# Unread products in front of the early attention steps: a number for each kind of step in place of one number for all

## The chip, the cores and the metric

The kernel runs on one core of a Trainium2 chip. The metric is the time of one execution on the device in microseconds (us), the median of several runs. TensorE (PE) does the matmuls, VectorE (DVE), ScalarE (ACT) and GpSimd (POOL) the elementwise work, SyncE (SP) issues most transfers. TensorE's clock is granted at one of two levels, 1.2 or 2.4 GHz; the profile shows it as 0.50 or 1.00.

## The reference

Eight batches of eight heads, 576 tokens each, head size 64. Each head gets two attentions, whose sum is the output: a pooled one over means of four tokens (144 x 144 scores), each result repeated four times, and a local one, in which a token sees those less than four places away. The heads side by side give 4608 tokens of 512 numbers, which go through two matrices with h * cos(h) between them.

```python
q_d = q.reshape(B, H, Sd, factor, D).mean(axis=3)      # the same for k and v; factor 4
out_up = np.repeat(sm_attn(q_d, k_d, v_d), factor, axis=2)
mask = np.abs(pos[:, None] - pos[None, :]) < factor
scores = np.where(mask, scale * q @ k.T, -1e9)         # softmax over the last axis -> attn
x = (out_up + attn @ v)                                # then (tokens, 512)
h = x @ w_in                                           # 512 -> 2048
return (h * np.cos(h)) @ w_out                         # 2048 -> 512
```

## The kernel before

Two heads make a pair, so a batch has four pairs; a pair goes through these steps on TensorE. `u_s` makes scores: local ones (L743 adds the mask through an identity, L748 multiplies small blocks of 32 x 32) and pooled ones (L757, L760). After a softmax on the other engines `u_t` transposes the pooled weights, in two halves (L829, L830). `u_pv` multiplies by the values: pooled (L975, 8 matmuls) and local (L987, many small matmuls of 24 columns). Float32 operands make two records of one such matmul in the trace.

The sums of both go into `x`, in tiles of 384 tokens; tile 0 needs batch 0 alone, tiles 1 and 2 need batch 1. Then `gemm1` multiplies a tile by one of 16 weight blocks (L1026, three float16 products for each of four parts of 512), `cosine` makes h * cos(h) on ScalarE and VectorE, and `gemm2` (L1132) accumulates the output. Before a weight block can be used, `w_split` splits it into two float16 halves (L477 to L485 on ScalarE and VectorE), with a sum over all partitions by four tiny matmuls (L499, L500). `x_scale` does the like for `x` (reduction into `vm` at L557, matmuls L560 and L561); it needs the squares of all values of batches 0 and 1.

Batches 0 and 1 are early: their attention runs before there are any products of tiles. The order of the work on every engine is written out by a planner: `schedule` lays each operation with a given length onto its engine by a key, forwards and backwards eight times, and `mend` then changes keys at random, from a fixed seed, and keeps what makes the plan shorter. An operation with alternatives goes to the engine that would be done sooner (the sums of pooled values `u_vd`, L701 and L702, to GpSimd or VectorE). So other lengths change the order on all engines.

TensorE gets products that nobody reads (L1279): identity times identity, 256 columns, into a bank that is free at the time. They stand in front of an operation where the plan has a gap, up to 16 of them. In front of every TensorE operation of an early attention step there are at least `CFG["warm"][batch]` of them, 2 for both batches, if a bank is free; the planner adds 0.11 us of planned length for each.

Of the kernel before, what the change touches and what calls it, by code (L numbers as in the profile page):

```python
# [52 lines left out]
NEARLY = 2  # L53
# [16 lines left out]


CFG = dict(cold=6.8, queue=0.0, alttol=0.3, iters=8, mix=0.0, tabpen=3.2, lat=0.2, latself=0.05, latpe=0.25, late=0.17,
           fgap=0.4, f0=0.8, fend=300.0, warm=(2, 2), fstep=0.13)


class Buf:
# [11 lines left out]

class Op:
    __slots__ = ("eng", "dur", "fn", "tab", "deps", "sdeps", "now", "start", "end", "lat", "name", "arg", "preds", "succs",  # L90
                 "i", "fin", "alts", "boost", "tol")


class Plan:
# [16 lines left out]
        i = self.turns[tag] = self.turns.get(tag, -1) + 1  # L111
        return f"{tag}.{i % n}"

    def op(self, eng, dur, fn, r=(), w=(), pw=(), tab=None, after=(), lat=0.0, alts=(), tol=None):
        o = Op()
        o.tol = CFG["alttol"] if tol is None else tol
        o.alts = {eng: (dur, fn)}
        for e, d, f in alts:
            o.alts[e] = (d, f)
        o.eng, o.dur, o.fn, o.tab, o.now, o.lat, o.name = eng, dur, fn, tab, self.now, lat, self.name  # L120
        o.arg, o.boost = self.arg, self.boost
        o.deps, o.sdeps = list(after), []
        if eng == "PE" and self.name in ("u_s", "u_t", "u_pv") and self.arg[0] < NEARLY:
            o.alts[eng] = (dur + 0.11 * CFG["warm"][self.arg[0]], fn)
        for b in r:
            o.deps += b.w
        for b in w:
            o.deps += b.r + b.w
        for b in pw:
            o.deps += b.r  # L130
        for b in r:
            b.r.append(o)
            b.acc.append(o)
        for b in w:
            b.w, b.r = [o], []
            b.allw.append(o)
            b.acc.append(o)
        for b in pw:
            b.w.append(o)
            b.allw.append(o)  # L140
            b.acc.append(o)
        self.ops.append(o)
        return o
# [210 lines left out]
def attn_ffn_kernel(ctx: ExitStack, tc: tile.TileContext, qT, kT, vdn, vl, w_in, w_out, out):  # L354
# [8 lines left out]
    pl = Plan()  # L363
# [44 lines left out]
    for t in range(NT):  # L408
        r = (t - TS) % (NX - 1)
# [195 lines left out]
    def h_scale(g, c0, c1, v):  # L605
# [6 lines left out]
        for c in range(c0, c1, n):  # L612
# [5 lines left out]
            for k in range(c, c + n):  # L618
# [14 lines left out]
                sml=([P, NBLK, BS], 4), smd=([P, NQG, SD], 3), ptd=([HD, 2, 2, SD], 2),  # L633
                xd=([P, SD], 2), xs=([P, S], 3))

    def ub(b, pr, name):
        return later(name, UNIT[name][0]) if b >= NEARLY and name in ("q", "k", "vl") else sb(name, UNIT[name][1], UNIT[name][0])
# [80 lines left out]
    def u_s(b, pr):  # L718
        pl.name = "u_s"
        u = st[(b, pr)]  # L720
        q, k_, qkd, qkg = u["q"], u["k"], u["qkd"], u["qkg"]
        early = b < NEARLY
        sml, smd = ub(b, pr, "sml"), ub(b, pr, "smd")
        banks = [bank(b, "s"), bank(b, "s")]
        loc, poo = pl.buf(None), pl.buf(None)
# [22 lines left out]
                            pe.matmul(to()[BS * w:BS * (w + 1), j - c.start], q.get()[hs, o:o + BS], k_.get()[hs, o:o + BS],  # L748
                                      start=not early, stop=not early or j == c.stop - 1)
        if early:  # L750
            pl.op("PE", 1.31, l_mm, r=[q, k_], pw=banks, w=[loc])

        def d_mm():
            to = [t() for _, _, _, t in cuts(gcut, SD)]
# [4 lines left out]
                hs = slice(64 * h, 64 * h + 64)  # L759
                pe.matmul(to[0][hs, 1], qkg()[hs, 0, SD - QG:], qkg()[hs, 1, :], start=True, stop=True)  # L760
        if early:
            pl.op("PE", 0.66, d_mm, r=[qkd], pw=banks, w=[poo])
        else:
            pl.op("PE", 1.62, lambda: (l_mm(), d_mm()), r=[q, k_, qkd], pw=banks, w=[loc, poo])

        n, m = NBLK * BS, NQG * SD
# [3 lines left out]
        for i, (k, c, w, src) in enumerate(cuts(lcut, BS)):  # L770
            if early:
                mx = pl.buf(None)
                using(k, "DVE", _dve(w), lambda c=c, src=src: dve.tensor_reduce(out=mxl.get()[:, c], in_=src(), axis=AX.X, op=ALU.max),
                      r=[loc], pw=[mxl], w=[mx])
                using(k, "DVE", _dve(w), lambda c=c, src=src: dve.tensor_tensor(
                    out=sml.get()[:, c], in0=src(), in1=wide(mxl.get()[:, c], BS), op=ALU.subtract), r=[loc, mx], pw=[sml])
            else:
                using(k, "DVE", _dve(w), lambda c=c, src=src: dve.tensor_tensor(out=sml.get()[:, c], in0=src(), in1=mask[:, c], op=ALU.add),
                      r=[loc], pw=[sml])
# [3 lines left out]
        for k, c, w, src in cuts(gcut, SD):  # L783
            using(k, "DVE", _dve(w), lambda c=c, src=src: dve.tensor_reduce(out=mxd.get()[:, c], in_=src(), axis=AX.X, op=ALU.max, negate=True),
                  r=[poo], pw=[mxd])
# [9 lines left out]
        o = pl.op("ACT", _act(n, False) + 1.2, exps, r=[poo], w=[mxd, sml, smd], pw=[su, part], tab="exp")  # L795
# [8 lines left out]
        for sm, f, size, bc in ((sml, sul, n, BS), (smd, sud, m, SD)):  # L804
            f = lambda e, sm=sm, f=f, bc=bc: lambda: e.tensor_tensor(out=sm.get(), in0=sm.get(), in1=wide(f(), bc), op=ALU.mult)
            alts = [("DVE", _dve(size), f(dve))]
# [8 lines left out]
    def u_t(b, pr):  # L815
        pl.name = "u_t"
        u = st[(b, pr)]
        sml, smd = u["sml"], u["smd"]
        ptd = ub(b, pr, "ptd")
        pl.op("DVE", _dve(NBLK * BS), lambda: dve.transpose(sml.get().rearrange("p c n -> p (c n)"), sml.get().rearrange("p c n -> p (c n)")),  # L820
              w=[sml])
        for kh in range(2):
            bk = bank(b, "t")

            def t_mm(kh=kh, bk=bk):
                ks = slice(kh * HD, (kh + 1) * HD)
                to = bk.get()[:HD, :2 * SD].rearrange("p (h n) -> p h n", h=2)
                for h in range(2):
                    pe.transpose(to[:, h, :SD - HQ], smd.get()[:SD - HQ, 2 * h, ks], ident[:SD - HQ, :SD - HQ])  # L829
                pe.transpose(to[:, :, SD - QG:], smd.get()[:, 1, ks], ident)  # L830
            pl.op("PE", 0.29, t_mm, r=[smd], w=[bk])
            evac(2 * SD, lambda kh=kh: ptd.get()[:, kh],
                 lambda bk=bk: bk.get()[:HD, :2 * SD].rearrange("p (a n) -> p a n", a=2), bk, ptd, scale=1.0)
        u["ptd"] = ptd
# [129 lines left out]
    def u_pv(b, pr):  # L964
        pl.name = "u_pv"
        u = st.pop((b, pr))
        sml, ptd, vd, vt, vdg = (u[n] for n in ("sml", "ptd", "vd", "vl", "vdg"))
        banks = [bank(b, "v") for _ in range(2)]
        poo, loc = pl.buf(None), [pl.buf(None) for _ in banks]
        xd, xs = ub(b, pr, "xd"), ub(b, pr, "xs")  # L970

        def d_mm():
            for kh in range(2):
                for h in range(2):
                    pe.matmul(banks[0].get()[64 * h:64 * h + 64, 2 * SD:3 * SD], vdg()[:, kh, 64 * h:64 * h + 64],  # L975
                              ptd.get()[:, kh, h, :], start=(kh == 0), stop=(kh == 1))
        if b < NEARLY:
            pl.op("PE", 0.64, d_mm, r=[vd, ptd], pw=[banks[0]], w=[poo])

        def l_mm():  # L980
            for a in range(NSEG // 2):
                for i in range(4):
                    for e in range(2):
                        for h in range(2):
                            r = slice(64 * h + 32 * e, 64 * h + 32 * e + 32)
                            o = (4 * a + i) * BQ
                            pe.matmul(banks[e].get()[64 * h:64 * h + 64, o:o + BQ], vt.get()[r, a, i, :], sml.get()[r, 4 * a + i, :BQ],  # L987
                                      start=True, stop=True)
        if b < NEARLY:
            pl.op("PE", 1.55, l_mm, r=[vt, sml], pw=banks, w=loc)  # L990
        else:
            pl.op("PE", 2.22, lambda: (d_mm(), l_mm()), r=[vd, ptd, vt, sml], pw=banks, w=loc + [poo])

        evac(SD, xd.get, lambda: banks[0].get()[:, 2 * SD:3 * SD], banks[0], xd, scale=0.25)
        xd.w[-1].deps += poo.w
        half = [pl.buf(None) for _ in range(2)]
        for e in range(2):
            pl.op("DVE", _dve(S // 2), lambda e=e: dve.tensor_tensor(
                out=xs.get().rearrange("p (a e n r) -> p a e n r", e=2, a=NSEG // 2, r=4)[:, :, e],
                in0=banks[e].get()[:, :12 * BQ].rearrange("p (a n r) -> p a n r", a=NSEG // 2, r=4),  # L1000
                in1=xd.get().rearrange("p (a e n) -> p a e n", e=2, a=NSEG // 2)[:, :, e].unsqueeze(3).broadcast_to(
                    [P, NSEG // 2, BQ, 4]), op=ALU.add), r=[banks[e], loc[e], xd], pw=[xs], w=[half[e]])
        x_out(b, pr, xs)
# [178 lines left out]
    for c in range(NC):  # L1182
        for k, d in (("i", 0.0), ("o", 0.2)):
            t = need[c - c % NF] + 0.4 * (c % NF) if c >= NF else need[c]
# [3 lines left out]
    for k in blocks:  # L1188
        i = min(i for i, s in enumerate(steps) if s[2:] + (s[0] >= TS,) == k)
# [29 lines left out]
    for i in range(len(steps) + LAG):  # L1219
        if i < len(steps):  # L1220
            t, c, c0, c1 = steps[i]
# [47 lines left out]
    with tc.manual_schedule():  # L1269
        constants()  # L1270
        for o in order:
            if o.eng == "PE" and o.start < CFG["fend"]:

                ahead = o.name in ("u_s", "u_t", "u_pv") and o.arg[0] == 0
                s = (last, 0.0, idle) if ahead else spare(last, o.start)
                early = o.name in ("u_s", "u_t", "u_pv") and o.arg[0] < NEARLY
                n = min(int((o.start - s[0] - CFG["fgap"]) / (0.23 if last < 5 else CFG["fstep"])), 16) if s else 0
                for _ in range(max(n, CFG["warm"][o.arg[0]] if early and s else 0)):
                    pe.matmul(s[2].get()[:, :2 * P], ident_b, ident_b.unsqueeze(1).broadcast_to([P, 2, P]), start=True, stop=True)  # L1279
                last = o.start + o.dur  # L1280
            made = o.fn()
            if size.get(o):
                room = AHEAD
                for prior, n in reversed(under):
                    room -= n
                    if room < 0:
                        tc.add_manual_dep(made.ins, prior.name, sync, reason="bytes under way")
                        break
                under.append((made.ins, size[o]))
# [35 lines left out]
```

## Time and profile before

| | us |
|---|---|
| three runs | 966.94, 966.71, 965.43; median 966.71 |
| the profiled execution | 967.24 |
| its span, first to last instruction | 965.5 |
| TensorE busy | 940.7 (97%) |
| VectorE busy | 792.6 (82%) |
| ScalarE busy | 616.9 (64%) |
| GpSimd busy | 374.2 (39%) |
| mean granted clock | 0.972 |

Busy time counts an engine as busy while one of its instructions runs, at whatever clock. A matmul at 1.2 GHz is a busy TensorE just as one at 2.4, so the share of busy time hides half-speed stretches; the granted clock shows them.

### The profile page before, as it was taken

What the parts mean: (1) busy time and instruction counts of PE and PEld (TensorE: products, weight loads), DVE (VectorE), ACT (ScalarE), POOL (GpSimd) and SP (SyncE); (2) the same over time, 40 slices, a digit from 0 to 9 for tenths busy, and PEclk for the clock granted to TensorE, in tenths of its full rate; (3) what the DMA queues carried; (4) which work ended last, traced back from release to release, by engine and by line L of the source; (5) the groups of instructions that cost most, each with busy time, mean ns of one, the idle gap of its engine ahead of it and who ended that gap; (6) DMA issues with size and microseconds to landing.
All of it is one profiled execution on the core that took longest, in us unless ns stands there. A gap on an engine that the chain in (4) does not pass through costs nothing.

```text
span 965.5 us, 29154 instructions
## 1 busy us (share of the span) xinstructions
PE 940.7 (97%) x12209; PEld 622.1 (64%) x12209; DVE 792.6 (82%) x1643; ACT 616.9 (64%) x1326; POOL 374.2 (39%) x515
## 2 busy tenths in 40 slices
PE   7899899999999999999999999999999999999998
PEld 5667555555565655655677676677777777676774
DVE  6865899899877776789998799898798889887774
ACT  3633688889786666557486576675467576665543
POOL 4542378566532322357742344351122233321010
PEclk9775899999999999999999999999999999999999
DMA  7851498976554541220110241130121110000000
GB/s 230 235 166 47 123 230 236 250 194 132 140 126 101 121 97 43 75 67 26 43 51 26 75 112 42 55 84 13 43 76 43 60 52 2 1 35 2 33 2 33
DMA packets 42732, 84.98 MB, mean 88 GB/s; under 512 B 4136, under 2 KB 14632, under 8 KB 42600
## 3 DMA queue, kind: packets, MB, share of 16 engines
q1 hardware_dynamic: 36120, 69.15, 22.5%
q0 software_dynamic: 6480, 13.96, 9.5%
q8 instruction: 96, 1.57, 0.7%
q14 instruction: 36, 0.29, 0.1%
HBM read 65.01 MB, written 18.09 MB: 86 GB/s over the span
## 4 chain that ended last, share of the span: by engine, by line
PE 85%; DVE 8%; issue 2%; ACT 2%; DMA 1%; POOL 0%; POOLq 0%; ACTq 0%; DVEq 0%; SPq 0%
PE bank L1132 34%; PE bank L1065 19%; PE bank L1026 13%; PE bank L987 5%; PE bank L748 3%; PE bank L1279 3%; PE bank L975 2%; PE bank L757 1%; DVE wv L483 1%; PE bank L829 1%; PE bank L760 1%; DVE wv L485 1%; DMA norm<-vdn 1%; PE bank L830 1%; DVE wv L481 1%
## 5 line engine op out<-in xcount | busy, mean ns | idle before, releaser
L1132 PE MATMUL bank<-wo,gh 128*128 128x512 f16 x996 | 296.2, 379 | 0.0
L443 POOL TENSOR_TENSOR gl<-tr,gh 128x384 f16<-128x384 f32 x92 | 93.3, 1014 | 248.3 <-ACT gh L1113 161.5
L1132 PE MATMUL bank<-wo,gl 128*128 128x512 f16 x498 | 188.6, 379 | 0.0
L1071 DVE TENSOR_TENSOR room<-room,bank 128x384 f32<-128x384 f32 x224 | 111.3, 499 | 46.3 <-PE bank L1065 38.3
L1132 PEld LDWEIGHTS <-gh 128*128 128x128 f16 x996 | 94.1, 98 | 77.1 <-issue 1.4
L1026 PEld LDWEIGHTS <-wi 128*128 128x128 f16 x960 | 94.5, 99 | 70.2 <-issue 4.3
L1065 PEld LDWEIGHTS <-wi 128*128 128x128 f16 x1344 | 114.7, 98 | 16.5 <-issue 1.0
L1110 ACT ACTIVATE tr<-tr,bhalf 128x384 f32<-128x384 f32 x166 | 100.5, 611 | 28.3 <-DVE tr L1108 26.3
L1065 PEld LDWEIGHTS <-room 128*128 128x128 f16 x1008 | 86.1, 98 | 17.8 <-issue 3.8
L1113 ACT ACTIVATE gh<-tr 128x384 f16<-128x384 f32 x128 | 66.1, 519 | 47.9 <-DVE tr L1111 33.9
L1132 PEld LDWEIGHTS <-gl 128*128 128x128 f16 x498 | 48.7, 98 | 58.8
L1111 DVE SCALAR_TENSOR_TENSOR tr<-tr,rho016True,room 128x384 f32<-128x384 f32 x112 | 74.1, 667 | 3.4 <-ACT tr L1110 2.4
L1026 PE MATMUL bank<-x0h,wi 128*128 128x384 f16 x256 | 69.9, 336 | 0.1
L1107 ACT ACTIVATE tr<-room,bquart,hs3016True 128x384 int32<-128x384 f32 x48 | 33.5, 704 | 43.4 <-DVE room L1071 43.1
L987 PEld LDWEIGHTS bank<-sml,vl 32*64 32x64 f32 x3072 | 53.3, 144 | 9.7 <-issue 6.3
L987 PE MATMUL bank<-sml,vl 32*64 32x24 f32 x3072 | 57.0, 220 | 2.2 <-issue 1.1
L1132 PE MATMUL bank<-wo,room 128*128 128x512 f16 x234 | 56.1, 379 | 0.0
L443 POOL TENSOR_TENSOR room<-room 128x256 f16<-128x256 f32 (+3 forms) x50 | 44.3, 928 | 24.8 <-ACT room L912 15.8
L443 DVE TENSOR_TENSOR gl<-tr,gh 128x384 f16<-128x384 f32 x74 | 47.0, 640 | 4.3 <-ACT gh L1113 2.9
L1107 ACT ACTIVATE tr<-room,bquart,hs2016True 128x384 int32<-128x384 f32 x48 | 33.0, 702 | 23.4 <-DVE room L1071 20.2
L1158 POOL DMA_DIRECT2D out<-ob x33 | 30.8, 1083 | 40.3 <-ACT ob L1149 20.5
L1279 PE MATMUL bank<-ident_b 128*128 128x256 bf16 x225 | 41.1, 314 | 3.7 <-POOL ident_b masks.py:199 3.7
(338 smaller groups left out, 2282.4 us busy)
## 6 DMA issues: line engine op xcount, KB each, us to landing
vl<-vl SPq DMA_DIRECT2D x32, 384.0 KB, 3.5
q<-qT SPq DMA_DIRECT2D x32, 292.0 KB, 4.0
k<-kT SPq DMA_DIRECT2D x32, 292.0 KB, 3.6
out<-ob SPq DMA_DIRECT2D x36, 256.0 KB, 2.1
out<-ob POOLq DMA_DIRECT2D x33, 256.0 KB, 6.7
wd<-w_in SPq DMA_DIRECT2D x16, 512.0 KB, 5.2
wd<-w_out SPq DMA_DIRECT2D x16, 512.0 KB, 4.7
norm<-vdn SPq DMA_DIRECT2D x24, 288.0 KB, 6.0
```

The source lines that it names most:

```text
L443: f = lambda e: lambda: e.tensor_tensor(out=out(), in0=in0(), in1=in1(), op=ALU.subtract)
L987: pe.matmul(banks[e].get()[64 * h:64 * h + 64, o:o + BQ], vt.get()[r, a, i, :], sml.get()[r, 4 * a + i, :BQ], start=True, stop=True)
L1026: pe.matmul(ph.get()[:, :m], w[:, i, kc, :], x[:, kc, :], start=(n == 0), stop=(n == 3 * KC - 1))
L1065: pe.matmul(to.get(), blk(a)[:, kc], x_parts(t)[b][0 if main else 1][:, i, kc], start=(n == 0), stop=(n == 5))
L1071: pl.op("DVE", _dve(n * HT), lambda: dve.tensor_tensor(out=out(), in0=wide(one.get()), in1=two(), op=ALU.add), r=r, w=w)
L1107: pl.op("ACT", _act(m, True, 2), lambda: act.activation(ti(), h(), AF.Identity, bias=bquart, scale=inv()), r=mine + [hp], w=[tr])
L1110: pl.op("ACT", _act(m, False, 1), lambda: act.activation(tr.get(), tr.get(), AF.Sin, scale=2.0 * PI, bias=bhalf), w=[tr], tab="sin")
L1111: pl.op("DVE", _dvs(m), lambda: dve.scalar_tensor_tensor(out=tr.get(), in0=tr.get(), scalar=rho(), in1=h(), op0=ALU.mult, op1=ALU.mult), r ...
L1113: pl.op("ACT", _act(m, False), lambda: act.activation(gh.get(), tr.get(), AF.Copy), r=[tr], w=[gh], alts=[("DVE", _dve(m / 2), lambda: dve ...
L1132: pe.matmul(o, (gh, gh, gl)[k].get()[:, sl], wo.get()[:, (0, 1, 0)[k]], start=(c == c0 and k == 0), stop=(c == c1 - 1 and k == 2))
L1158: pl.op("POOL", 1.0, lambda dst=dst, ob=ob: pool.dma_start(dst, ob.get(), accum_op=ALU.add), r=[ob], w=[part[(t, i)]], lat=6.0)
L1279: pe.matmul(s[2].get()[:, :2 * P], ident_b, ident_b.unsqueeze(1).broadcast_to([P, 2, P]), start=True, stop=True)
```

## The change

The number of unread products now hangs on the kind of step and no longer on the batch: local scores 2 (`l`), pooled scores 1 (`d`), each half of the transposes 1 (`t`), pooled values 1 (`vd`), local values 4 (`vl`). An operation carries its number as `warm`, and the planner adds the same 0.11 us for each. A pair had 12 at least and has 9. Gaps in the plan are filled as before.

```diff
-           fgap=0.4, f0=0.8, fend=300.0, warm=(2, 2), fstep=0.13)
+           fgap=0.4, f0=0.8, fend=300.0, fstep=0.13)
+WARM = {"l": 2, "d": 1, "t": 1, "vd": 1, "vl": 4}
...
-        if eng == "PE" and self.name in ("u_s", "u_t", "u_pv") and self.arg[0] < NEARLY:
-            o.alts[eng] = (dur + 0.11 * CFG["warm"][self.arg[0]], fn)
+        if warm:
+            o.alts[eng] = (dur + 0.11 * warm, fn)
...
-            pl.op("PE", 1.31, l_mm, r=[q, k_], pw=banks, w=[loc])
+            pl.op("PE", 1.31, l_mm, r=[q, k_], pw=banks, w=[loc], warm=WARM["l"])
...
-            pl.op("PE", 0.29, t_mm, r=[smd], w=[bk])
+            pl.op("PE", 0.29, t_mm, r=[smd], w=[bk], warm=WARM["t"] if b < NEARLY else 0)
...
-            pl.op("PE", 1.55, l_mm, r=[vt, sml], pw=banks, w=loc)
+            pl.op("PE", 1.55, l_mm, r=[vt, sml], pw=banks, w=loc, warm=WARM["vl"])
...
-                early = o.name in ("u_s", "u_t", "u_pv") and o.arg[0] < NEARLY
                 n = min(int((o.start - s[0] - CFG["fgap"]) / (0.23 if last < 5 else CFG["fstep"])), 16) if s else 0
-                for _ in range(max(n, CFG["warm"][o.arg[0]] if early and s else 0)):
+                for _ in range(max(n, o.warm if s else 0)):
```

In the order of instructions the line numbers of the changed kernel are two or three higher (L1281 for L1279, L990 for L987). TensorE, batch 1, where the first product of tile 0 stands (`x0h` and `wi` are its operands, `wq` the sums of weight block 1, `sml` and `vl` local values, `ptd` and `vsum` pooled ones). Before:

```order
L987 MATMUL bank<-sml,vl 64x24 x48
L499 MATMUL bank<-wq,ones 128x2
L500 MATMUL bank<-ones,tiny 128x2
...
L829 MATMUL bank<-ident,smd 72x96 x2
L830 MATMUL bank<-ident,smd 72x2x64
L1026 LDWEIGHTS wi_1040
L1026 MATMUL bank<-x0h,wi_1040 128x384
```

And now, from the last matmul of that product on:

```order
L1029 LDWEIGHTS wi_1044
L1029 MATMUL bank<-x0h,wi_1044 128x384
L502 MATMUL bank<-wq,ones 128x2
L503 MATMUL bank<-ones,tiny 128x2
...
L990 MATMUL bank<-sml,vl 64x24 x48
L1281 LDWEIGHTS ident_b
L1281 MATMUL bank<-ident_b 128x256
L978 MATMUL bank<-ptd,vsum 64x144 x4
```

The last pair's local values and the sums of block 1 stood ahead of the product, and stand behind it now; the pooled values of that pair stand behind it in both.

VectorE in batch 0, up to the reduction into `vm` (`wd` and `vsum` are the sums of pooled values of one pair). Before:

```order
L820 STREAM_TRANSPOSE sml<-sml 128x384
L701 TENSOR_TENSOR wd<-wd 72x512
L702 TENSOR_TENSOR vsum<-wd 72x256
L651 COPY ptd<-bank 72x288
L651 TENSOR_SCALAR xd<-bank 128x144
L701 TENSOR_TENSOR wd<-wd 72x512
L702 TENSOR_TENSOR vsum<-wd 72x256
L998 TENSOR_TENSOR xs<-bank,xd 128x3x96
L557 TENSOR_REDUCE vm<-vq_126 128x1
```

And now:

```order
L654 COPY ptd<-bank 72x288
L823 STREAM_TRANSPOSE sml<-sml 128x384
L704 TENSOR_TENSOR wd<-wd 72x512
L705 TENSOR_TENSOR vsum<-wd 72x256
L654 TENSOR_SCALAR xd<-bank 128x144
L560 TENSOR_REDUCE vm<-vq_126 128x1
```

Two pairs of batch 1 were summed here on VectorE, now it is one; the other stands on GpSimd. The first sum of `xs` stands behind the reduction now.

## Rows read from the trace of the kernel before

**Rows 1.** The page's forty slices: PE busy in tenths, granted clock in tenths.

```profile
PE   7899899999999999999999999999999999999998
PEclk9775899999999999999999999999999999999999
```

**Rows 2.** Stretches: length, busy of PE, PEld, DVE, ACT, POOL, clock, DMA.

```profile
34.70:44.90 10.20, 9.47 (x188) 7.34 (x188) 8.59 (x23) 4.36 (x12) 6.45 (x11) 0.50 0.82 241
44.90:48.30 3.40, 3.14 (x102) 2.26 (x94) 1.58 (x4) 1.41 (x4) 0.94 (x3) 1.00 0.86 259
48.30:55.10 6.80, 6.74 (x185) 4.68 (x178) 6.30 (x14) 2.47 (x5) 6.33 (x10) 0.50 0.71 232
55.10:65.40 10.30, 8.42 (x220) 6.18 (x220) 8.53 (x35) 4.53 (x18) 4.42 (x7) 1.00 0.74 229
65.40:75.60 10.20, 9.93 (x82) 6.09 (x83) 3.87 (x13) 3.94 (x16) 1.26 (x3) 0.50 0.02 5
75.60:79.00 3.40, 3.40 (x154) 2.75 (x154) 1.83 (x6) 1.15 (x7) 0.44 (x1) 1.00 0.02 5
79.00:99.50 20.50, 19.19 (x302) 13.16 (x297) 9.86 (x28) 6.80 (x17) 4.74 (x10) 0.50 0.16 54
99.50:113.20 13.70, 9.52 (x76) 6.84 (x75) 12.20 (x31) 8.28 (x17) 2.49 (x7) 1.00 0.31 83
```

**Rows 3.** Chain of waits, 35.4 to 101 us: start, length, what.

```profile
63.05 1.88 issue
...
76.31 1.64 PE bank L987 x96
...
79.29 0.83 issue
...
84.24 0.43 PE bank L1279 x2
84.67 2.70 PE bank L987 x96
...
95.93 3.78 PE bank L1026 x12
...
100.68 0.30 ACT xd L650
```

**Rows 4.** TensorE's timeline: start, length of the group, what.

```profile
30.15 0.33 PE L829 MATMUL bank<-ident,smd 96*72 96x96 f32 x2
...
30.43 0.38 PE L1279 MATMUL bank<-ident_b 128*128 128x256 bf16 x2
...
65.94 0.61 PE L1279 MATMUL bank<-ident_b 128*128 128x256 bf16 x2
66.61 0.54 PE L829 MATMUL bank<-ident,smd 96*72 96x96 f32 x2
...
67.15 0.63 PE L1279 MATMUL bank<-ident_b 128*128 128x256 bf16 x2
...
101.06 0.33 PE L1026 MATMUL bank<-x0h,wi 128*128 128x384 f16 x1
...
103.01 1.91 PE L1279 MATMUL bank<-ident_b 128*128 128x256 bf16 x16
```

**Rows 5.** Two further stretches, columns as in rows 2.

```profile
18.10:35.40 17.30, 13.70 (x371) 10.25 (x369) 17.13 (x38) 13.05 (x39) 11.94 (x11) 0.98 0.81 224
...
65.94:99.93 33.99, 32.41 (x500) 21.70 (x495) 15.55 (x45) 12.07 (x39) 6.43 (x12) 0.56 0.10 34
```

**Rows 6.** VectorE's timeline before the reduction into vm.

```profile
32.71 0.67 DVE L701 TENSOR_TENSOR wd<-wd 72x512 f32<-72x512 f32 x1
33.42 1.44 DVE L702 TENSOR_TENSOR vsum<-wd 72x256 f32<-72x256 f32 x1
...
35.16 0.14 DVE L557 TENSOR_REDUCE vm<-vq 128x1 f32<-128x8 f32 x1
```

More of the change, by code (lines that the diff above doesn't have):

```diff
@@ L90 @@
     __slots__ = ("eng", "dur", "fn", "tab", "deps", "sdeps", "now", "start", "end", "lat", "name", "arg", "preds", "succs",
-                 "i", "fin", "alts", "boost", "tol")
+                 "i", "fin", "alts", "boost", "tol", "warm")
 class Plan:
@@ L112, in turn, with op @@
         return f"{tag}.{i % n}"
-    def op(self, eng, dur, fn, r=(), w=(), pw=(), tab=None, after=(), lat=0.0, alts=(), tol=None):
+    def op(self, eng, dur, fn, r=(), w=(), pw=(), tab=None, after=(), lat=0.0, alts=(), tol=None, warm=0):
         o = Op()
+        o.warm = warm
         o.tol = CFG["alttol"] if tol is None else tol
@@ L761, in u_s @@
         if early:
-            pl.op("PE", 0.66, d_mm, r=[qkd], pw=banks, w=[poo])
+            pl.op("PE", 0.66, d_mm, r=[qkd], pw=banks, w=[poo], warm=WARM["d"])
         else:
@@ L977, in u_pv @@
         if b < NEARLY:
-            pl.op("PE", 0.64, d_mm, r=[vd, ptd], pw=[banks[0]], w=[poo])
+            pl.op("PE", 0.64, d_mm, r=[vd, ptd], pw=[banks[0]], w=[poo], warm=WARM["vd"])
         def l_mm():
```

## The prediction

> **What bounds the kernel now.** I read the page's row of slices first, then a table of stretches cut where the clock changes, then the chain of waits, then TensorE's own timeline. The slices show TensorE (PE) busy nine tenths or more nearly everywhere, and the granted clock below ten tenths in slices 2 to 5 only, the first 120 us [rows 1]. So what the change can move lies there; behind it the rows of products stand in much the same order. The stretches say where the clock was at its lower level of 1.2 GHz: 34.7 to 44.9, 48.3 to 55.1, 65.4 to 75.6 and 79.0 to 99.5 us, 47.7 us in all, with PE busy for 45.3 of them (9.47 + 6.74 + 9.93 + 19.19) [rows 2]. PE is not starved there, it runs at half speed. From 35.4 to 100.6 us the chain of waits is made of PE pieces, with a few stops called issue in which PE waited for nothing that the profile shows (1.88 us at 63.05, 0.83 us at 79.29); at 100.68 it goes over to ScalarE, and behind it VectorE (DVE) [rows 3]. Before 35.4 it is DVE, busy 17.13 us in 17.30 [rows 5].
>
> What a step costs at either level: the local values of one pair (96 records of L987) took 2.70 us at half clock and 1.64 at full, which is 1.65 times and not twice, and an unread product 0.43/2 = 0.215 us at half [rows 3]; at full clock 16 of them took 1.91 us, 0.12 us each. The score transposes of one step, from their start to that of the product behind them, took 67.15 - 66.61 = 0.54 us at half and 30.43 - 30.15 = 0.28 at full; one first product (L1026, 12 matmuls) took 1.95 us at full (101.06 to 103.01) [rows 4] and 3.78 us at half [rows 3].
>
> **What the change does.** Fewer products stand before most steps and four before the local values, but gaps in the plan are filled up to 16 as before: the total is 225 in both orders. So it isn't the sum that changes, it is the place, and with the changed planned lengths the order of steps on all engines. I go by stretches.
>
> *From the last local scores to the end of the first product of tile 0 (65.9 to 99.9 us).* Between them 33 products stand in the order before and 27 now: 6 x 0.215 = 1.3 us less at half clock.
>
> *The first product of tile 0 goes ahead of the last pair's values.* Before, the local values of pair 3 and the sums of weight block 1 run first, at half clock, and the clock rises only at 99.5, when the 12 dense matmuls are through [rows 2, 3]. Now they come behind the dense product and should find a risen clock. Values 2.70 - 1.64 = 1.06 us less; five unread products there in place of two, 3 x 0.12 = 0.36 us more; the weight sums, four tiny matmuls, are set at nothing. Together -0.7 us. Nothing that DVE needs sooner is held up: tile 0 needs batch 0 alone.
>
> *The clock.* Unknown, so bounded from both sides. As far as it can help: the clock stays up from its rise at 55.1. The two stretches after 65.4 are 10.2 + 20.5 = 30.7 us [rows 2] and would shrink by 1 - 1/1.65, 12.1 us. As far as it can hurt there: the only stretch at full clock between 65.4 and 99.5, 75.6 to 79.0, is lost, 3.4 x 0.65 = 2.2 us. What the rows say of its reasons: it fell at 79.0 after 3.40 us of PE busy in 3.40, nearly all of it local values with two pairs of unread products [rows 2, 3]. [...] In the new order the densest place of this part is where pair 2 is finished: two transposes with one product each, three before the pooled values, four before the local values, nine in all, whereas before it were two at each. I take it that the clock rises there, one pair earlier than at 99.5, and holds into the dense product. Then at full clock: local values of pair 2 -1.06; the two transposes of pair 3, 2 x (0.54 - 0.28) = -0.52; the dense product 3.78 - 1.95 = -1.83; four unread products 4 x 0.095 = -0.4; sum -3.8. Against it stands the lost stretch, +2.2. Net -1.6 us. I choose this between +2.2 and -12.1 because the nearest row, 75.6, shows a rise after just such a bunch.
>
> The Trainium skill, TensorE: Matmul & The Clock Gate, section "Why this matters for your kernels", has the clock fall when gaps between bursts of matmuls grow too long, so that busy matmuls would keep it up; by that rule alone the two arrangements would cost the same but for their places. The trace differs: the fall at 79.0 followed 3.40 us busy in 3.40.
>
> *VectorE ahead of the scale of x (28 to 35.4 us).* DVE added up pooled values of two pairs of batch 1 just before the reduction into vm; now one pair stands there and the other goes to GpSimd. One such sum took 0.67 us in its first half and 1.44 in its second, and vm began at 35.16 [rows 6]. If all of it shows, -2.1 us; if ScalarE's squares, which vm also reads, are late, nothing; if the sum that is now GpSimd's holds up the pair 3 behind it on GpSimd, the same 2.1 us more. I take half, -1.0, since DVE is the chain there [rows 5].
>
> *From 35 to 65 us* PE's steps and their products are nearly the same (16 and 16 before two of the steps in both). I set this at 0; at most it gives back half-clock time, (10.2 + 6.8) x 0.39 = 6.6 us, which data and DVE (8.59 of 10.20 us busy) allow in part only, or loses the full stretch 44.9 to 48.3, 3.4 x 0.65 = 2.2 us [rows 2].
>
> *What passes on.* A product that PE finishes earlier frees DVE earlier: DVE was busy 15.55 of 33.99 us between 65.94 and 99.93 [rows 5], so it has room for all of -3.6. Behind 100 us DVE takes over as the chain and simply starts sooner. The stops at issue stay, set at 0; if a faster PE meets another of the larger kind it costs 1.88 us, if both go it gains 2.7 [rows 3].
>
> **Sum.** -1.3 - 0.7 - 1.6 - 1.0 = -4.6 us. The profiled execution took 967.24 us (its span of 965.5 and 1.7 around it), so 962.6; the median of the runs is 0.5 lower, 966.71, and so I forecast 962.1.
>
> **Rivals.** *The clock holds.* Four products ahead of the values were the missing part, and it stays up from 55.1. For it: those values are the largest steps at half clock. Against it: the stop of 1.88 us at 63.05 lies in the last local scores, before a fall at 65.4, and nothing in the change takes that stop away. Time: 12.1 instead of 1.6, with the 0.7 contained in it and the fewer products worth 0.7 at full clock: 966.7 - 12.1 - 0.7 - 1.0 = 952.9.
>
> *VectorE eats it.* The chain from 100.6 on is DVE, busy 12.20 of 13.70 us [rows 2]. If the new order puts the splitting of weights, which then decides, no earlier on DVE, PE's gain turns into a longer wait for the sums of block 2. Against it: DVE's 15.55 of 33.99. Time: 966.7, less or more 1.
>
> *The clock is lost (slower).* Products are taken from transposes, pooled scores and pooled values, and PE falls to 1.2 GHz in stretches that ran at full clock. Place: batch 0's transposes and values between 24 and 34.7, and the two short full stretches. Price: 10.3 x 0.65 = 6.7 us in the first, of which I let half show, since DVE is the chain there, 3.3; 2 x 2.2 in the other two; less 1.3 + 0.7 of the terms that remain: +5.7, so 972.4. It decides the sign from where more than the 3.0 us of the first, second and fourth terms is lost. For it: 65.4 to 75.6 began with transposes and a pair of products at each, and stayed low. Against it: over batch 0's steps 31 products stood before and 35 now. The same page, section "Part 4: PE-mode transpose", says that a transpose doesn't count as busy for the clock like another matmul. By that rule one product beside a transpose is too little, and this rival gains; the trace agrees so far as four products around the first step's transposes, at 65.94 and 67.15, brought no rise [rows 2, 4].
>
> **Chances and range.** The forecast 0.42 (own range 958 to 965), the clock holds 0.22, VectorE eats it 0.15, slower 0.21. A difference under 0.2%, 1.9 us, can't be told from none in this kernel. Faster: 0.42 less 0.02, 0.22, and 0.02 of the third, 0.64; same: 0.02 and 0.13, 0.15; slower 0.21. The range goes from the clock that holds nearly all of the way, 953.5, to a loss half as large as the third rival's and a little more, 970.0.
>
> **What would show it.** Right: PE's clock at 2.4 GHz from the values of pair 2 on, a start of vm before 34.5, the end of the first dense product three to four us before 99.9. Wrong: the clock at 1.2 GHz as long as before (47.7 us up to 99.5), or at 2.4 throughout; a wait of PE before the sums of block 2 longer by as much as was gained; or a fall before 34.7 us.

## The result

| | before | changed |
|---|---|---|
| runs, same chip | 4: 965.43 to 971.54 us | 4: 952.35 to 956.46 us |
| median | 966.83 us | 954.69 us |
| ratio | | 0.9864, 95% interval 0.9824 to 0.9905 |
| profiled execution (its span) | 967.24 (965.5) us | 955.54 (953.8) us |
| mean granted clock in it | 0.972 | 0.985 |

The change made the kernel faster, by 1.4% here, and by more than forecast: 954.69 us against 962.1. The four runs of before were on the high side. Beside the experiments below, on three chips, before ran 93 times more; the 84 of these runs that the comparisons use have a median of 962.2 us (953.0 to 970.3), and against that the gain is about 7.5 us. This sets runs of different chips side by side; e1 below, which took as long as the changed kernel, gained 8.5 us on its own chip (954.69 against 963.19). The ratios and the table leave out runs more than 1.5% above the fastest of the same kernel, but a lost clock alone can put a run there, so the last column of the table counts all runs, as the medians of the experiments in the text do.

The slices of the changed kernel, PE busy and clock in tenths, against [rows 1]:

```profile
PE   8898999999999999999999999999999999999998
PEclk9779899999999999999999999999999999999999
```

In slice 4, from 72 to 95 us, the clock is now at 9 where it was at 5; slices 2, 3 and 5 stand at 7, 7 and 8 as before. PE is about as busy as it was, and what changed is its speed while it is busy. The same stretches as in [rows 2], with the same columns:

```profile
34.70:44.90 10.20, 9.35 (x195) 7.13 (x195) 9.94 (x23) 8.24 (x24) 6.62 (x10) 0.61 0.72 225
44.90:48.30 3.40, 3.40 (x59) 2.49 (x49) 1.15 (x3) 0.13 (x1) 1.49 (x2) 0.50 0.84 257
48.30:55.10 6.80, 6.74 (x156) 4.71 (x158) 5.93 (x14) 1.47 (x3) 5.19 (x9) 0.50 0.74 233
55.10:65.40 10.30, 9.73 (x269) 7.19 (x262) 7.94 (x30) 4.75 (x18) 6.00 (x10) 0.89 0.73 239
65.40:75.60 10.20, 9.79 (x298) 7.20 (x298) 7.53 (x23) 4.79 (x20) 2.53 (x3) 1.00 0.20 58
75.60:79.00 3.40, 3.28 (x61) 2.07 (x55) 2.86 (x5) 1.96 (x5) 1.88 (x2) 1.00 0.00 0
79.00:99.50 20.50, 16.33 (x281) 12.87 (x274) 20.30 (x57) 13.73 (x30) 4.83 (x13) 0.89 0.27 87
99.50:113.20 13.70, 13.70 (x78) 8.02 (x76) 12.91 (x33) 12.21 (x23) 5.60 (x11) 0.92 0.79 249
```

From 65.4 to 75.6 us PE is as busy as before (9.79 us against 9.93) and gets further. The counts, 298 records and 82, don't measure by how much: 190 of the 298 are the short matmuls of local values, of which before had none in this stretch. Cut where its own clock changes, the trace has one low stretch up to 57.4 us and a short one from 94.9:

```profile
36.90:57.40 20.50, 19.66 (x391) 14.19 (x385) 17.12 (x43) 7.64 (x18) 13.78 (x21) 0.50 0.75 237
57.40:65.40 8.00, 7.43 (x193) 5.45 (x195) 5.64 (x19) 4.75 (x18) 3.86 (x7) 1.00 0.70 231
...
79.00:94.90 15.90, 12.95 (x264) 9.95 (x256) 15.90 (x43) 10.32 (x23) 3.69 (x9) 1.00 0.20 69
94.90:101.80 6.90, 5.68 (x28) 4.56 (x29) 6.48 (x20) 5.71 (x12) 2.34 (x7) 0.51 0.59 178
```

So the early low stretches are no shorter (20.5 us, 17.0 before), and the 30.7 us between 65.4 and 99.5 are gone but for the last 4.6. VectorE is the busy one now: 15.90 us in 15.90. The chain of waits of the changed kernel (start, length, what) says the same, against [rows 3]:

```profile
64.75 0.57 issue
...
74.22 1.58 PE bank L990 x92
75.82 0.30 ACT xd L653
76.14 0.46 DVE xs L1001
...
78.18 0.82 issue
79.01 0.41 DVE wv L484
79.42 1.20 DVE wv L486 x2
...
95.34 0.73 ACT wd L494 x2
96.12 0.59 PE bank L502 x2
```

The chain leaves PE for ScalarE and VectorE at 76 us, not at 100. From there it is mostly VectorE: the sums of `xs` and the splitting of weights. The stop in the last local scores is 0.57 us, not 1.88. PE's timeline has the first dense product (its first and last row), the start of the second, and the sums of block 2:

```profile
81.65 0.32 PE L1029 MATMUL bank<-x0h,wi 128*128 128x384 f16 x1 [0.28 <-DVE xs L1001]
...
83.43 0.33 PE L1029 MATMUL bank<-x0h,wi 128*128 128x384 f16 x1
...
88.42 0.33 PE L1029 MATMUL bank<-x0h,wi 128*128 128x384 f16 x1
...
96.12 0.59 PE L502 MATMUL bank<-wq,ones 128*128 128x2 f32 x2 [3.83 <-ACT wd L494]
```

And the sums of block 2 before:

```profile
107.76 0.38 PE L499 MATMUL bank<-wq,ones 128*128 128x2 f32 x2 [2.84 <-ACT wd L491]
```

The first product ends near 83.7 us; before it ended at 95.93 + 3.78 = 99.7 [rows 3], 16.0 us later. But part of that is order: the last pair's local values and the sums of block 1 stood ahead of it and stand behind it now. At the second product PE has done the same steps in both; it starts at 88.42 us, and started at 101.06 [rows 4]. So PE gained 12.6 us. What PE waits for (in total, times, longest):

```profile
PE bank L502 <- ACT wd L494: 3.8, 1, 3.8
PE bank L563 <- DVE vm L560: 1.9, 1, 1.9
```

And before, in the same stretch of 30 to 115 us:

```profile
PE bank L499 <- ACT wd L491: 4.1, 2, 2.8
...
PE bank L975 <- DVE vm L557: 1.5, 1, 1.5
```

The longest wait for the sums of a block, those of block 2, is 3.8 us (2.8 before). They start at 96.12 us, and started at 107.76, 11.6 us later, and the span is 11.7 us shorter: of the 12.6 us that PE gained, 1.0 went into a longer wait for the splitting of weights.

### The profile page after: what moved, and what is told of

The parts are those of the page before. It is cut to its first block, busy times and chain, and to the rows that moved or that the text cites. A ratio compares the mean times of both kernels' runs of the same rounds, so it can differ in the third digit from the quotient of the medians.

```text
span 953.8 us, 29147 instructions
## 1 busy us (share of the span) xinstructions
PE 930.0 (98%) x12209; PEld 617.3 (65%) x12209; DVE 793.3 (83%) x1653; ACT 616.1 (65%) x1323; POOL 375.0 (39%) x512
## 3 DMA queue, kind: packets, MB, share of 16 engines
q8 instruction: 96, 1.57, 0.7%
## 4 chain that ended last, share of the span: by engine, by line
PE 79%; DVE 13%; DMA 4%; ACT 1%; issue 1%; POOL 1%; POOLq 0%; DVEq 0%; ACTq 0%
PE bank L1135 33%; PE bank L1068 20%; PE bank L1029 10%; PE bank L990 4%; PE bank L751 3%; PE bank L1281 2%; PE bank L978 2%; DMA wd<-w_out 2%; DVE wv L486 1%; PE bank L760 1%; PE bank L763 1%; DMA out<-ob 1%; DVE room L446 1%; PE bank L832 1%; DVE wv L488 1%
## 5 line engine op out<-in xcount | busy, mean ns | idle before, releaser
L446 POOL TENSOR_TENSOR gl<-tr,gh 128x384 f16<-128x384 f32 x89 | 88.3, 993 | 259.6 <-ACT gh L1116 157.8
L1135 PEld LDWEIGHTS <-gh 128*128 128x128 f16 x996 | 94.0, 98 | 77.3 <-issue 2.0
L1113 ACT ACTIVATE tr<-tr,bhalf 128x384 f32<-128x384 f32 x166 | 100.2, 611 | 27.1 <-DVE tr L1111 25.4
L1114 DVE SCALAR_TENSOR_TENSOR tr<-tr,rho016True,room 128x384 f32<-128x384 f32 x112 | 72.0, 649 | 3.5 <-ACT tr L1113 2.9
L1029 PE MATMUL bank<-x0h,wi 128*128 128x384 f16 x256 | 67.5, 326 | 0.3 <-DVE xs L1001 0.3
L990 PEld LDWEIGHTS bank<-sml,vl 32*64 32x64 f32 x3072 | 49.5, 136 | 7.6 <-issue 5.5
L990 PE MATMUL bank<-sml,vl 32*64 32x24 f32 x3072 | 53.1, 215 | 0.6 <-issue 0.4
L1281 PE MATMUL bank<-ident_b 128*128 128x256 bf16 x225 | 40.6, 312 | 4.2 <-POOL ident_b masks.py:199 3.7
L808 POOL TENSOR_TENSOR smd<-smd,su 128x432 f32<-128x432 f32 x16 | 15.2, 952 | 68.7 <-DVE su L806 62.3
```

Source lines behind the costliest of these rows:

```text
L446: f = lambda e: lambda: e.tensor_tensor(out=out(), in0=in0(), in1=in1(), op=ALU.subtract)
L1029: pe.matmul(ph.get()[:, :m], w[:, i, kc, :], x[:, kc, :], start=(n == 0), stop=(n == 3 * KC - 1))
L1113: pl.op("ACT", _act(m, False, 1), lambda: act.activation(tr.get(), tr.get(), AF.Sin, scale=2.0 * PI, bias=bhalf), w=[tr], tab="sin")
L1114: pl.op("DVE", _dvs(m), lambda: dve.scalar_tensor_tensor(out=tr.get(), in0=tr.get(), scalar=rho(), in1=h(), op0=ALU.mult, op1=ALU.mult), r ...
L1135: pe.matmul(o, (gh, gh, gl)[k].get()[:, sl], wo.get()[:, (0, 1, 0)[k]], start=(c == c0 and k == 0), stop=(c == c1 - 1 and k == 2))
```

## The experiments

The planned lengths (`WARM`) and the products really issued are one table in the changed kernel. In all kernels below they are two, so that the order of the work and the dealing of the products can be set apart; none leaves out a part of the computation. What they change is short:

```diff
-                for _ in range(max(n, o.warm if s else 0)):
+                for _ in range(max(n, o.floor if s else 0)):
+WARM  = {...}    # planned lengths: sets the order on all engines
+FLOOR = {...}    # products issued at least
+MOVES = [...]    # single TensorE steps put behind another
+EXTRA = {...}    # at least so many products in front of one step
```

The table has, beside the time, the *missing clock*: (1 - mean granted clock) x span, the mean over the runs, and how many runs had a mean clock of 0.983 or more. Such a run is said below to keep the clock; where in the program a run lost it, the mean doesn't say.

| | order | products | runs | median us | missing clock | 0.983 or more | of all runs |
|---|---|---|---|---|---|---|---|
| before, beside them | old | 225 | 84 | 962.2 | 21.9 us | 7 of 84 | 7 of 93 |
| changed | new | 225 | 4 | 954.7 | 12.9 | 4 of 4 | 4 of 4 |
| e1 | new | 234 | 6 | 954.7 | 10.5 | 6 of 6 | 6 of 6 |
| e2 | old | 213 | 12 | 964.9 | 25.4 | 0 of 12 | 0 of 12 |
| e3 | new | 201 | 3 | 955.0 | 12.4 | 3 of 3 | 3 of 6 |
| e4 | new | 214 | 8 | 958.5 | 15.8 | 5 of 8 | 5 of 12 |
| k1 | old, 2 moves | 225 | 10 | 962.2 | 20.4 | 3 of 10 | 3 of 12 |
| k3 | new, 1 move | 234 | 12 | 962.2 | 19.2 | 0 of 12 | 0 of 12 |
| k4 | old | 241 | 11 | 961.4 | 19.7 | 4 of 11 | 4 of 12 |
| k5 | old lengths, other seed | 241 | 7 | 959.0 | 15.2 | 6 of 7 | 6 of 12 |
| k6 | new lengths, other seed | 245 | 12 | 957.6 | 12.2 | 12 of 12 | 12 of 12 |
| k7 | old, 2 moves | 237 | 11 | 961.1 | 19.5 | 2 of 11 | 2 of 12 |
| k8 | old | 237 | 12 | 961.4 | 18.9 | 4 of 12 | 4 of 12 |
| k9 | new | 256 | 10 | 957.3 | 11.0 | 10 of 10 | 11 of 12 |

A straight line through these 202 runs, with one slope for all and a height of its own for each kernel, gives 0.69 us of span for 1 us of missing clock (what is left scatters by 1.6 us), and heights from 943.0 to 947.7: before 945.3, changed 943.9 (four runs alone, so by that scatter good to 0.8 us). By this line 9.0 us less missing clock are worth 6.2 of the 7.5 us. The question is what keeps the clock.

**The order or the dealing.** e1 has the order of the change and two products in front of every step, as before had:

```diff
+FLOOR = {"l": 2, "d": 2, "t": 2, "vd": 2, "vl": 2}   # WARM as in the change
```

> The order of steps on every engine is that of the changed kernel; only the unread products actually issued go back to at least two in front of every early step (234 in all instead of 225). Theory A (the four products in front of local values hold the clock): local values have two again, the clock falls again between 65 and 99 us, and the time returns by at least half of the gain, 960 to 965 us. Theory B (the order that the planner made from the changed lengths holds it, the products matter little): 954 to 957 us, the 9 products more costing about 1 us at 0.12 us each; the clock stays at 2.4 GHz from 57 us to 95 us as in the changed kernel.

Measured: 954.69 us, ratio to before 0.9902 (0.9868 to 0.9937). e2 is the reverse, the order of before and the dealing of the change:

```diff
+WARM  = {"l": 2, "d": 2, "t": 2, "vd": 2, "vl": 2}
+FLOOR = {"l": 2, "d": 1, "t": 1, "vd": 1, "vl": 4}
```

> The order of steps on every engine is that of the kernel before; only the unread products issued are dealt out by kind (2, 1, 1, 1, 4; 213 in all instead of 225). Theory A: most of the gain comes with the products alone, 954 to 959 us, the clock at 2.4 GHz for most of 55 to 99 us. Theory B: the old order keeps its falls, 963 to 968 us, the clock low for over 35 us of the first 100.

Measured: 964.93 us, ratio 1.0005 (0.9975 to 1.0034). So the new dealing gives nothing in the old order, and the new order gives the whole gain with two products everywhere. In the stretches of e2's one trace (columns as above) the low clock of before has only another place:

```profile
57.00:75.20 18.20, 15.91 (x461) 11.60 (x462) 14.56 (x44) 9.57 (x39) 7.12 (x10) 1.00 0.37 117
75.20:92.30 17.10, 16.63 (x263) 11.82 (x257) 8.55 (x24) 6.80 (x17) 3.62 (x9) 0.50 0.21 65
```

**How many products the new order needs.** e3 has one in front of local values, e4 one there and two at each half of the transposes:

```diff
+FLOOR = {"l": 2, "d": 1, "t": 1, "vd": 1, "vl": 1}   # e3
+FLOOR = {"l": 2, "d": 1, "t": 2, "vd": 1, "vl": 1}   # e4
```

> The changed kernel's order, one product instead of four at least in front of local values (201 in all). Theory A: without them the clock falls as before, 959 to 965 us. Theory B: 953 to 955 us, the 24 products less being worth up to 2 us.

> The changed kernel's order, about as many products, but those taken from local values stand at the transposes (2 at each half, 1 at local values; 214 in all). Theory A, that they have to stand before local values: 959 to 965 us. Theory B, and also that only their number counts: 953 to 957 us.

Measured: e3 959.76 us, ratio 0.9889 (0.9839 to 0.9939); e4 960.2, ratio 0.9945 (0.9913 to 0.9976). Over all runs both medians lie where theory A put them, and the two kernels keep the clock in 8 of 18 runs, where the changed kernel, e1 and k9, in the same order, keep it in 21 of 22. So the order is not enough by itself, and the dealing isn't without effect. Whether it is one product in front of local values that is too few, or the smaller number in all, these runs don't separate: the kernels with one there are also those with the fewest products (201 and 214, against 225 and more).

**Local values of two pairs in a row.** In the order of before the clock fell at 79.0 us in local values of two pairs with two products between them; in the new order other steps stand there. k3 takes the new order of e1 and moves one step, the local values of pair 0 of batch 1, right in front of pair 1's. k1 takes the old order and parts the pairs:

```diff
+MOVES = [(287, 295)]               # k3, WARM and FLOOR as in e1
+MOVES = [(296, 276), (320, 381)]   # k1, WARM and FLOOR 2 for all
```

> The changed kernel's order with two unread products at every early step (as in the run with 954.7 us), but for one step on TensorE: the local values of pair 0 of batch 1 are moved back to stand directly before those of pair 1, as in the kernel before. Theory C: the clock falls at that place in a part of the runs, 957 to 963 us. Theory D: 953 to 956 us.

> The kernel before in all but two places on TensorE: the local values of pair 1 of batch 1, which followed those of pair 0 directly, stand behind the first half of pair 2's transposes, and those of pair 3 behind the first dense product of tile 0, as in the changed kernel. The number of unread products is the same, 225. Theory C (two pairs' local values next to each other lose the clock, and the new order keeps them apart): 954 to 960 us, the clock at 2.4 GHz over most of 57 to 95 us. Theory D (the whole order, with shorter waits of TensorE, does it): 961 to 966 us, at most the 1 to 2 us of the values that now run behind the dense product.

Measured: k3 962.2 us, ratio 0.9999 (0.9975 to 1.0024), so this one move costs the whole gain of e1. Two rows of k3's stretches and its chain between them:

```profile
65.40:77.30 11.90, 10.80 (x285) 7.61 (x279) 8.45 (x27) 5.24 (x22) 2.67 (x4) 1.00 0.15 46
77.30:87.50 10.20, 10.20 (x132) 7.19 (x132) 7.26 (x14) 5.09 (x15) 1.74 (x2) 0.50 0.02 5
```

```profile
72.98 0.34 PE bank L992 x20
73.31 0.33 PE bank L1299 x2
73.64 0.83 PE bank L992 x42
74.47 0.56 issue
75.03 1.00 PE bank L992 x54
```

The second pair's 96 local values, with a stop of 0.56 us in them, follow the first's with two products between and end at 76.0 us, and the clock falls at 77.3, in the transposes behind them. Then 10.2 us at 1.2 GHz follow, all of them busy. k1: 963.41 us, ratio 0.998 (0.994 to 1.0019). Its one profiled execution kept the clock from 55.7 us to the end, in a span of 950.6 us:

```profile
65.40:75.60 10.20, 9.47 (x242) 6.90 (x242) 7.77 (x20) 5.07 (x21) 3.58 (x5) 1.00 0.09 29
75.60:79.00 3.40, 3.34 (x131) 2.51 (x123) 2.75 (x6) 2.43 (x7) 0.55 (x1) 1.00 0.02 7
79.00:94.90 15.90, 11.95 (x182) 8.85 (x182) 13.35 (x37) 9.84 (x25) 4.07 (x9) 1.00 0.21 68
```

Most of its other runs didn't (3 of all 12 at 0.983 or more). The trace alone would have settled for the wrong story: what one execution shows of the clock isn't what the kernel does on average. Standing apart is not enough.

k4 leaves the old order and puts ten products, in place of two, between the two pairs' values; k5 is the kernel before with another seed of the planner's search, as a measure of chance:

```diff
+EXTRA = {296: 10, 320: 10}          # k4
-random.Random(1)                    # k5
+random.Random(2)
```

> The kernel before with 10 instead of 2 unread products at two steps only: in front of the local values of pair 1 and of pair 3 of batch 1, which stand right behind other values there (241 in all). They cost 16 x 0.12 = 1.9 us at full clock. Theory C: they break the run of values and pay, 954 to 960 us. Theory D: 964 to 968 us, their own cost and no more.

> The kernel before with another seed of the planner's random search, so another order of about the same planned quality, and the lengths and numbers of before (2 each). If the order that falls out decides (luck of the plan), the time differs from before by several us either way, 954 to 967; if the changed lengths by themselves lead to a better order, this one stays at 961 to 966 us.

Measured: k4 961.55 us, ratio 0.9986 (0.9953 to 1.0018), no gain. k5 961.07, ratio 0.997 (0.9937 to 1.0002). Its runs fall into two groups, seven from 956.3 to 962.4 us and five from 971.5 to 975.5 at a mean clock of 0.971 or less; the clock is kept in six of the twelve, and the ratio counts the first group alone.

**The fetch stop and the values together.** A second suspect was the stop in the last local scores, 1.88 us in before. In ten traces up to then the clock fell behind it in three of the four where it took 1.6 us or more, and in none of the six where it took 1.05 or less; in k6, run after that, it took 1.57 us and the clock held. The DMA view of before, for 62.6 to 63.8 us, has one packet of the queue that the profile calls instruction:

```profile
q8 instruction: 1, 0.02, 5.2%
```

It landed at 63.67 us, and PE went on at 64.92. In all fourteen traces the timelines from 8 to 130 us show 40 stops of PE put down to issue, and each ended 0.87 to 1.65 us after such a packet had landed. So the name fetch stop has support; which engine's instructions a packet holds, the traces don't say. k8 puts 14 products in front of these scores in the old order, k7 does that and parts the values as k1 does. k9 has the new order with more products, as the candidate to beat both; k6 the change with the other seed:

```diff
+EXTRA = {241: 14}                                    # k8; k7 with k1's MOVES
+FLOOR = {"l": 2, "d": 2, "t": 2, "vd": 2, "vl": 4}   # k9, and EXTRA = {241: 8}
-random.Random(1)                                     # k6, the change otherwise
+random.Random(2)
```

> The plan of before, order unchanged, with 14 unread products instead of 2 in front of the last local scores alone; 237 in all. Theory F: the fall of the clock at 65 us goes, that in the local values of two pairs (79.0) stays, so about half of the gain, 957 to 962 us. If the fetch stop has no part in it: 963 to 967. If it is the only cause: 952 to 956.

> The plan of before, with two edits: the local values of pairs 1 and 3 stand apart from those of pairs 0 and 2, and 14 unread products (instead of 2) stand in front of the last local scores, where the fetch of instructions stopped TensorE for 1.88 us at 63.05; 237 unread products in all (before 225). Theory F (before loses its clock after 57 us for two causes, the fetch stop in the last local scores and the local values of two pairs in a row): both are taken away, so the clock holds from about 56 us in most runs, some 8 to 12 us less low clock; 952 to 957 us. Theory B (it is the order of the whole plan of the new lengths, not these two places): 960 to 966.

Measured: k8 961.34 us, ratio 0.9971 (0.9939 to 1.0003). Its chain shows that the products took the stop's place:

```profile
63.58 1.64 PE bank L1299 x14
65.21 0.11 PE bank L748
65.32 0.43 PE bank L753 x34
65.75 0.03 issue
65.78 0.45 PE bank L753 x27
```

0.03 us of stop are left of 1.88, and the clock held over this place and over the values of the two pairs, to fall for 3.4 us at 85.0, where the dense product starts:

```profile
57.60:65.40 7.80, 7.80 (x171) 5.73 (x173) 6.06 (x22) 4.62 (x18) 1.20 (x3) 1.00 0.70 205
65.40:75.60 10.20, 9.90 (x288) 7.08 (x281) 6.86 (x19) 5.08 (x21) 3.65 (x4) 1.00 0.21 63
75.60:79.00 3.40, 3.19 (x112) 2.34 (x104) 3.40 (x9) 1.60 (x5) 1.88 (x2) 1.00 0.02 7
79.00:85.00 6.00, 5.74 (x202) 4.43 (x195) 4.38 (x12) 3.64 (x10) 1.01 (x2) 1.00 0.31 86
85.00:88.40 3.40, 3.40 (x14) 1.60 (x12) 2.53 (x11) 1.63 (x3) 2.35 (x6) 0.50 0.48 166
```

This execution took 955.4 us; eight of the twelve took 961 to 966. k7, with both suspects gone, should have come to 952 to 957: it took 961.75, ratio 0.9971 (0.9936 to 1.0005), two runs of twelve with the clock. So the theory that these two places are the cause of before's loss fell. The values can cost the clock, as k3 shows, and the four kernels that change these places in the old order (k1, k4, k7, k8) keep it oftener than before, in 13 of 48 runs against 7 of 93; but taking both away doesn't give it back. Where k7 lost it isn't seen: its one trace is of an execution of 1204.96 us at a granted clock of 0.75 or less throughout, for a reason that no run shows.

> The changed kernel with another start of the planner's random search: the same lengths and the same dealing, another order; 245 unread products. If the new lengths as such make the plan better (they keep local values apart and bring the first products early): 951 to 957 us. If the gain is one order that the search happened to find: anywhere from 953 to 968, 962 as likely as not.

> The plan of the change, with two unread products in front of each early step, four in front of local values, and 8 in front of the last local scores; 256 in all (after 219). Theory F: the clock holds as in the changed kernel and oftener, 951 to 955 us. Theory that the unread products cost their time where VectorE isn't ahead: 37 more products of about 0.23 us at full clock are at most 8.5 us, 955 to 963.

Measured: k6 957.59 us, ratio 0.9962 (0.9931 to 0.9992); k9 957.43, ratio 0.9941 (0.9908 to 0.9973). k6 keeps the clock in every run although its order is another one, and although two pairs' local values stand side by side in it too, with four products between. But its height is 947.7 against 943.9, and it ends 2.9 us behind the changed kernel. k9 keeps the clock in 11 of 12 runs (one of the eleven took 2399.48 us, for a reason that no run shows). It has 256 - 225 = 31 more products (the expectation had 37 at 0.23 us each, which is nearer to the price at half clock) and a height of 947.5, 3.6 us more; 0.12 us for each would make 3.7, but that the products are the reason isn't shown, and k6 with 20 more is as high. Nothing tried beats the changed kernel beyond doubt; e1 equals it.

**What stays open.** Which property of the new order keeps the clock isn't settled. The order is needed, and the new dealing without it gives nothing (e1, e2); one moved step can undo it (k3), and so, in half of the runs, can fewer products (e3, e4). Of the old lengths one seed loses the clock mostly (7 of 93 keep it) and another in half of its runs (k5), and both seeds keep it with the new lengths, so that the new lengths are better for it, and not merely two lucky draws, is likely but not shown. The old and the new order differ before 57 us too, and what that part does for the clock behind it wasn't tested apart.

## Why the prediction was partly right

The sign and the range were right, and the place, 65 to 100 us at TensorE. The size was not, and the forecast's account of the clock was not what happened.

**Fewer products (-1.3) and the dense product first (-0.7).** The 27 products are in the trace, between 65.4 and 83.6 us, and the dense product does run ahead of the last pair's local values, which come at 84.6 us at full clock. Both happened, but both were worked out at the clock of before, and are small parts of what the clock gave.

**The clock (-1.6).** This is the step that failed. I took it that the clock would be lost as before and rise one pair earlier. In the trace it was not lost at all between 57.4 and 94.9 us. Of the signs named, the clock at 2.4 GHz throughout that stretch is one of being wrong. The rival "the clock holds" came true: its 12.1 us are near the 12.6 that PE gained in the two traces, and its 952.9 us lies 1.8 below the median measured. That it came so close is in part luck: it stands on runs of before that were on the high side, and against the 84 others the whole gain is 7.5 us. Against it I had named the stop of 1.88 us, of which "nothing in the change takes that stop away". It went with the order or the dealing, or differs by itself: in the changed kernel's trace it is 0.57 us, in e1 0.59, and in e2, in the old order, 1.05, with one trace of each. So a stop is no fixed cost of a place in the program. For it I had named the four products in front of local values, and that reason was wrong too: e1 has two and keeps the clock, e2 has four and loses it. Only one, in e3 and e4, goes with a clock that is lost in 10 of 18 runs. Nor does the row that the fall at 79.0 was read from repeat itself: in k8's trace the same two pairs' values, with two products between them, ran at full clock from 72.94 to 76.7 us. A forecast from the rows of one execution could not have told this; what could be seen was that a bounded unknown from +2.2 to -12.1 us was by far the largest term, and a rise one pair earlier was chosen in it on a single row. The rule of gaps that the prediction weighed (the Trainium skill, TensorE: Matmul & The Clock Gate, section "Why this matters for your kernels") doesn't settle it either. The trace of the changed kernel agrees at 94.9 us, where the clock fell in the wait of 3.83 us that ends at 96.12, and the trace of before doesn't at 79.0, where it fell after 3.40 us of PE busy in 3.40.

**VectorE before vm (-1.0).** VectorE's timeline of the changed kernel before the reduction, against [rows 6]:

```profile
33.29 0.69 DVE L704 TENSOR_TENSOR wd<-wd 72x512 f32<-72x512 f32 x1 [2.47 <-ACT wv L699]
34.01 0.42 DVE L705 TENSOR_TENSOR vsum<-wd 72x256 f32<-72x256 f32 x1
...
34.57 0.15 DVE L560 TENSOR_REDUCE vm<-vq 128x1 f32<-128x8 f32 x1
```

The reduction starts at 34.57 us, 0.59 earlier than at 35.16. The one sum that is left waited 2.47 us for ScalarE first. And PE waited 1.9 us for vm; the 1.5 of before stand at pooled values (L975), which don't read vm. The term was 0.6 at most, and nothing of it is left at the last local scores (the next point).

**35 to 65 us set at nothing.** Right: the last local scores end at 66.3 us, 65.9 before, with 20.5 us of low clock instead of 17.0.

**"DVE has room for all of it."** Right for the 3.6 us meant, and nearly so for 12.6: VectorE is busy in all of 79.0 to 94.9 us, and the rival "VectorE eats it" took 1.0 us at the sums of block 2, as a small part of the account and not as its end.

**Slower through a lost clock.** Didn't happen; batch 0's steps kept the clock to 36.9 us, longer than before's 34.7. Its price took 10.3 us for a place, 24 to 34.7, that is 10.7 long, which moves its time by 0.2 us at most.

## What to carry to other kernels

When an unread filler is dealt out anew and a planner sees it as length, two things change at once, and the order can be the one that counts more: measure the two apart, as e1 and e2 do, before crediting the filler. A clock that is lost in some runs needs many runs; a single profiled execution shows how a loss looks, not how often it comes (k1, k8). And of a sum in which one unknown spans 14 us and the rest comes to 3, the forecast is that unknown, and a value inside it needs more than one row behind it.

## What the runs showed of the hardware

- The same kernel, before, took from 953.0 to 970.3 us, and most of this spread is the granted clock: 0.69 us of span for each us of missing clock, with a remaining scatter of 1.6 us.
- A stop of PE put down to issue, in the same step of the program, took 0.03 us (k8), 0.57 (changed), 1.05 (e2), 1.88 (before) and 2.41 (k4). Fourteen products in front of it filled the time. 40 of 40 such stops ended 0.87 to 1.65 us after a packet of the instruction queue had landed.
- TensorE stayed at 1.2 GHz through 10.20 us of busy time in 10.20 (k3, 77.3 to 87.5 us): transposes, pooled and local values, unread products and most of a dense product.
